# The output projection of the first two units of a retention and SwiGLU kernel, as seven products of halves

## The chip, the cores and the metric

The kernel runs on one core of a Trainium2 chip. The metric is the device time of one execution in microseconds. Before the change the median of three runs is 1154.93 us (1154.29 to 1156.06). The profile is of one more execution, with a span of 1155.2 us. A granted TensorE clock of 0.993 of full speed goes with it.

## What is computed

Eight batches of eight heads run retention over 576 positions of 64 dimensions. The result, as 4608 tokens of 512, goes through RMSNorm and a SwiGLU block of width 1536. All is float32, except that the weights arrive as float64.

```python
ret = (q @ k.T / sqrt(64)) * Dmat          # decay gamma[h] ** (i - j), causal
x = (ret @ v) -> (4608, 512)               # per batch and head, then joined
xn = x / sqrt(mean(x * x) + 1e-6) * rms_g
out = (silu(xn @ w_gate) * (xn @ w_val)) @ w_out
```

## The kernel before

**Units and pairs.** The tokens are cut into 12 units of `U` = 384. The retention is done for 32 pairs of heads; `slot(j)` holds the small matmuls of pair j (`values`, `scores`, `states`, `carried`) with VectorE's `weigh` and `sums`. Units 0 and 1 need pairs 0 to 7, which `start()` does first. From unit 2 on a main loop does, for each unit, six groups of gate and val projections (`up`), and in the last group and after it the output projection `across`, with the slots of later pairs placed between them.

**Seven products for eight.** From unit 2 on every large matrix product is taken over halves in the manner of Strassen and Winograd: seven products of halves, with sums of blocks of the activations (VectorE) and of the weights made beside them. The weight blocks are named A11, A12, A22, and S1 to S4 for combinations of quarters. For gate and val the combinations are made once, by `combine(m)` on GpSimd (L812 to L819), in `w_up[m]`, which has room for 14 block columns. For the output projection they are made by `combine_out` on VectorE, stored in DRAM as `w_blocks`, and fetched into four slots in `w_out`, in the order A11, S1, S3, S2, A12, S4, A22, as `across` needs them (`fetch`, `ORDER`).

**Units 0 and 1 are plain.** While they run, the weights still arrive as float64 and are turned into float32 by a sequence of VectorE and ScalarE steps (`rounding`, by chunks; the chunks of `w_out` are the last). `up_plain` (L554 to L573) does gate and val of both units in full products of 384 columns: four matmuls to a bank, then ScalarE's silu for gate or VectorE's multiplication into `h` for val (L570). The hidden values of unit 1 lie in `w_up[1][:, 8:]`, in the columns that `combine(1)` later overwrites with S2, S3 and S4 of val. `down(u, s)` (L575 to L584) then makes 128 tokens of the output at a time: twelve matmuls of 512 columns, a ScalarE copy, one contiguous store of 256 KB.

**The order around the change.** It is written out by hand, and each engine works its own part of it in that order: at the end of `start()`, `following(7)` (transposes of pair 8 on VectorE, loads of pair 9), stores of A11, A12 and A22, `combine(0)`, three times `down(1, s)` with the three steps of normalising unit 2 between them (`norm_0`, `norm_1` with `diagonals`, `norm_2`), `combine(1)`, `slot(8, rest=False)`, `following(8)`, three times `down(0, s)`, `slot(9)`, `following(9)`. `values(j)` ends with a tiny GpSimd memset (`tick`, L359), for which the first matmul of `carried(j)` waits. `combine_out` is spread over the 42 steps of unit 2's `up`, one operation of 128x256 to a step, 24 in all; the stores of S1, S3, S2 and S4 and the first four fetches follow it.

**`across(u)`** first makes two blocks of h on VectorE (L649: t1 = b12 - b11, then b12 = b22 - b12), 1152 columns each. Then it does product after product, each 2 x 6 matmuls of 192 columns: A11 by b11, S1 by t1, S3 by b12, S2 by b11 + b12, A12 by b21, S4 by b22, A22 by b21 less the sum. The results are added on VectorE (L646), turned by 32x32 transposes (L659) into one of three output buffers, and stored in eight transfers of 24 KB each. Its four banks come from the pool of five.

Of the kernel before, what the change touches and what calls it, by code (L numbers as in the profile page):

```python
# [14 lines left out]
P = 128  # L15
# [26 lines left out]
def kernel(  # L42
# [21 lines left out]
    U = 384  # L64
# [22 lines left out]
    def bank(name):  # L87
        return banks.tile([P, 512], F32, tag="b", name=name)
# [483 lines left out]
                    nc.scalar.activation(out=h, in_=ps[:, :U], func=AF.Silu)  # L572
                yield  # L573

    def down(u, s):  # L575
        ps = bank(f"out_{u}_{s}")
        for f in range(NF):
            nc.tensor.matmul(  # L578
                ps[:, :DM], lhsT=h_of[u][:, f, s * P : s * P + P], rhs=w_out[:, f],
                start=(f == 0), stop=(f == NF - 1),  # L580
            )
        o = outs.tile([P, DM], F32, tag="o", name=f"o_{u}_{s}")
        nc.scalar.copy(out=o, in_=ps[:, :DM])
        nc.sync.dma_start(out=out[u * U + s * P : u * U + s * P + P, :], in_=o)  # L584


    ORDER = (A11, S1, S3, S2, A12, S4, A22)
    DH = DM // 2
    w_blocks = dram.tile([7, P, NH, DH], F32, name="w_blocks")
    w_slots = w_out.rearrange("p f d -> p (f d)").rearrange("p (s f d) -> p s f d", s=4, d=DH)  # L590
    n_fetched = 0

    def quarter(row, col):

        return w_out[:, col * NH : col * NH + NH, row * DH : row * DH + DH]

    def keep(blk, t):
        nc.sync.dma_start(out=w_blocks[blk], in_=t)

    def combine_out():  # L600

        a11, a12, a21, a22 = (quarter(r, c) for r in range(2) for c in range(2))
        for c in range(NH):
            for o, a, b, op in (
                (a22, a21, a22, ALU.add), (a21, a11, a21, ALU.subtract),
                (a11, a22, a11, ALU.subtract), (a12, a12, a11, ALU.subtract),
            ):
                nc.vector.tensor_tensor(out=o[:, c], in0=a[:, c], in1=b[:, c], op=op)
                yield
        for blk, t in ((S1, a22), (S3, a21), (S2, a11), (S4, a12)):  # L610
            keep(blk, t)
        for _ in range(4):
            fetch()

    def fetch():
        nonlocal n_fetched
        if n_fetched < 7 * (NU - 2):
            nc.sync.dma_start(
                out=w_slots[:, n_fetched % 4], in_=w_blocks[ORDER[n_fetched % 7]]
            )  # L620
            n_fetched += 1

    def across(u):


        h = h_of[u]
        b11, b12 = h[:, :NH, :HU], h[:, :NH, HU:]
        b21, b22 = h[:, NH:, :HU], h[:, NH:, HU:]
        t1 = ffn.tile([P, NH, HU], F32, tag="t1", name=f"t1_{u}")
        x_, y, z, w = (bank(f"{n}o_{u}") for n in "xyzw")  # L630
        s1, u2, u4 = (temp(f"{n}o_{u}") for n in ("m1", "u2", "u4"))

        def product(rhs, ps, start):
            k = 7 * (u - 2) + n_done
            for i in range(2):
                for c in range(NH):
                    nc.tensor.matmul(  # L637
                        ps[:, i * HU : i * HU + HU],
                        lhsT=w_slots[:, k % 4, c, i * P : i * P + P], rhs=rhs[:, c],
                        start=(start and i == c == 0), stop=False, skip_group_check=True,  # L640
                    )
            if n_done < 3:
                fetch()

        def add(o, a, ps):
            nc.vector.tensor_tensor(out=o, in0=a, in1=ps[:, :U], op=ALU.add)  # L646

        def block(o, a, b, op):
            nc.vector.tensor_tensor(out=o, in0=a, in1=b, op=op)  # L649

        def result(row, col, a, ps):
            r = ps[:, :U]
            if a is not None:
                r = temp(f"c{row}{col}_{u}")
                add(r, a, ps)
            o = outs.tile([P, DM], F32, tag="o", name=f"o_{u}_{row}_{col}")[:, :U]
            end = u == NU - 1
            if not end:
                nc.vector.transpose(out=o, in_=r)  # L659
            o_of = o.rearrange("p (d t r) -> p d t r", d=2, r=SQ)  # L660
            for d in range(2):
                if end:
                    half = slice(d * HU, d * HU + HU)
                    nc.vector.transpose(out=o[:, half], in_=r[:, half])
                for i in range(P // SQ):
                    c0 = row * DH + d * P + i * SQ
                    t0 = u * U + col * HU
                    queue = nc.scalar if end and i % 2 else nc.sync
                    queue.dma_start(
                        out=out[t0 : t0 + HU, c0 : c0 + SQ].rearrange("(t c) r -> c t r", c=SQ),  # L670
                        in_=o_of[i * SQ : i * SQ + SQ, d],
                    )

        n_done = 0
        block(t1, b12, b11, ALU.subtract)
        block(b12, b22, b12, ALU.subtract)
        yield
        product(b11, x_, True)
        nc.scalar.copy(out=s1, in_=x_[:, :U])
        block(b11, b12, b11, ALU.add)  # L680
        n_done += 1
        yield
        product(t1, z, True)
        n_done += 1
        yield
        product(b12, w, True)
        n_done += 1
        yield
        product(b11, y, True)
        add(u2, s1, y)  # L690
        add(u4, u2, z)
        result(1, 1, u4, w)
        n_done += 1
        yield
        product(b21, x_, False)
        result(0, 0, None, x_)
        block(b21, b21, b11, ALU.subtract)
        n_done += 1
        yield
        product(b22, z, False)  # L700
        result(0, 1, u2, z)
        n_done += 1
        yield
        product(b21, w, False)
        result(1, 0, u2, w)
        yield
# [146 lines left out]
    def start():  # L853
# [52 lines left out]
        gather(*squares.pop())  # L906
        load_qk(2 * NHP)
        load_kv(2 * NHP)
        for m, g in [(m, g) for g in range(NG) for m in range(2)]:
            for u in range(2):  # L910
                weights_to(4 * g + 2 * m + 1)
                for i, _ in enumerate(up_plain(u, m, g)):
                    if not (u or m or g):
                        if i == 0:
                            values(2 * NHP - 1)
                            carried(2 * NHP - 1)
                            gather(1, NHP - 1, square(1, NHP - 1))
                        elif i == 1:
                            norm_1(1)
                        elif i == 2:  # L920
                            diagonals(1)
                        elif i == 3:
                            norm_2(1)
                    weights(2)
                    act(1)
                    if i == 1:
                        weights_to(4 * g + 2 * m + 2)
        following(2 * NHP - 1)
        weights_to(len(chunks))
        for blk, row, col in ((A11, 0, 0), (A12, 0, 1), (A22, 1, 1)):  # L930
            keep(blk, quarter(row, col))
        combine(0)
        for u in (1, 0):
            for s in range(NS):
                down(u, s)
                if u == 1:
                    (norm_0, norm_1, norm_2)[s](2)
                    if s == 1:
                        diagonals(2)
            if u:  # L940
                combine(1)
                slot(8, rest=False)
                following(8)
        slot(9)
# [21 lines left out]
    with tc.manual_schedule():  # L966
        start()
        for u in range(2, NU):
            made = combine_out() if u == 2 else iter(())
            for i in range(2 * NG):  # L970
                for n, _ in enumerate(up(u, i % 2, i // 2)):
                    next(made, None)
                    if n == 2 and turns:
                        prepare_next(turns.pop())
                if u > 2 and i in (1, 3):
                    fetch()
                    fetch()
                if i == 2 * NG - 1:
                    rest = across(u)
                    next(rest)  # L980
                behind(u, i)
            for i, _ in enumerate(rest):
                if i == 0 and turns:
                    prepare_next(turns.pop())
                if i == 2:
                    behind(u, 6)
                    at, n = SLOTS[u % 3]
                    if 2 * NG - 1 in at:
                        load_next(u // 3 * 8 + n + len(at) - 1)
                elif i == 4:  # L990
                    behind(u, 7)
# [27 lines left out]
```

## Time and profile before

| what | where it is read | value |
|---|---|---|
| median time | three runs | 1154.93 us |
| TensorE matmul busy | page, part 1 | 1132.9 us of 1155.2 |
| matmul, 512 columns, `down` | groups by line, L578 | 593 ns each by the record, 72 to a unit |
| matmul, 192 columns, `across` | groups by line, L637 | 326 to 329 ns each by the record |
| VectorE block of h, 128x1152 | groups by line, L649 | 1342 ns |
| VectorE weight combination, 128x256 | groups by line, L608 | 416 ns, 24 of them |
| GpSimd weight combination | groups by line, L819 | 1340 ns (gate), 1303 ns (val), 12 each |
| store of a block to `w_blocks` | transfers | 768 KB, median 6.0 us to landing |

A float32 matmul of the program stands as two records in the profile. The records overlap, so a stage is measured from one start to the next rather than by the sum of the records. In the busy time by stage the columns are start and end in us, length, then busy time and instruction count of TensorE's matmuls, its weight loads, VectorE, ScalarE and GpSimd, the granted clock, the share of the transfer engines and GB/s. In the order of time the columns are start, length, engine, line and operation, and in brackets how long the engine was idle before and what ended it.

### The profile page before, as it was taken

The numbers are of one execution on the slowest core, as the hardware profiler recorded it, in microseconds if no ns is written. First come the engines' busy times: TensorE is split into PE (matmuls) and PEld (weight loads), VectorE is DVE, ScalarE is ACT, GpSimd is POOL, SyncE is SP. The second block draws the span as 40 slices with busy tenths as digits, with TensorE's granted clock in tenths as the row PEclk, the third lists the DMA queues.
The fourth block names the chain that finished last, engine by engine and source line by source line (L and its number), as shares of the span: only waits on it lengthen the run. The fifth ranks groups of instructions, "written<-read, shape, count | busy, mean of one in ns | idle before, by whom it ended". The sixth has DMA issues, their size and how long they took to land.

```text
span 1155.2 us, 24332 instructions
## 1 busy us (share of the span) xinstructions
PE 1132.9 (98%) x10332; PEld 1025.7 (89%) x10332; DVE 696.4 (60%) x1414; ACT 246.4 (21%) x484; POOL 46.5 (4%) x74
## 2 busy tenths in 40 slices
PE   7899999999999999999999999999999999999998
PEld 6655555459999999999999999999999999999998
DVE  3888864428676575465765775465576566445352
ACT  4645641111211221111221120120220220120210
POOL 0000005500000000000000000000000000000000
PEclk8899999999999999999999999999999999999999
DMA  7945322322972656034345456306336403303304
GB/s 199 270 98 172 109 84 65 110 68 43 268 156 42 173 132 150 20 95 111 96 102 90 109 135 132 115 26 120 101 97 140 128 34 94 126 1 98 122 1 110
DMA packets 282412, 125.37 MB, mean 109 GB/s; under 512 B 257216, under 2 KB 264896, under 8 KB 282304
## 3 DMA queue, kind: packets, MB, share of 16 engines
q1 hardware_dynamic: 272688, 108.71, 37.4%
q10 hardware_dynamic: 9616, 15.11, 4.0%
q8 instruction: 81, 1.33, 0.5%
q14 instruction: 27, 0.22, 0.1%
HBM read 108.83 MB, written 14.94 MB: 107 GB/s over the span
## 4 chain that ended last, share of the span: by engine, by line
PE 91%; DVE 4%; SPq 2%; issue 1%; ACT 1%; DMA 1%; DVEq 0%; POOL 0%; POOLq 0%
PE w L507 13%; PE x L507 13%; PE z L507 13%; PE up L564 11%; PE xo L637 7%; PE wo L637 7%; PE zo L637 7%; PE y L507 6%; PE out L578 5%; PE yo L637 3%; PE av L351 2%; PE s L280 1%; PE s L300 1%; PE av L370 1%; SPq L161 1%; DVE sum L329 1%
## 5 line engine op out<-in xcount | busy, mean ns | idle before, releaser
L531 ACT COPY m<-x 128x384 f32<-128x384 f32 x60 | 28.7, 478 | 431.4 <-PE x L507 407.6
L507 PE MATMUL w<-sums,w_val 128*128 128x192 f32 x480 | 88.6, 328 | 0.4
L507 PE MATMUL z<-x,w_gate 128*128 128x192 f32 x480 | 87.9, 326 | 1.0 <-DVE u L514 1.0
L507 PE MATMUL w<-sums,w_gate 128*128 128x192 f32 x480 | 88.0, 326 | 0.8 <-DVE h L514 0.8
L507 PE MATMUL x<-x,w_val 128*128 128x192 f32 x480 | 88.7, 328 | 0.0
L507 PE MATMUL x<-x,w_gate 128*128 128x192 f32 x480 | 88.5, 328 | 0.0
L507 PE MATMUL z<-x,w_val 128*128 128x192 f32 x480 | 87.8, 326 | 0.0
L637 PE MATMUL xo<-h,w_out 128*128 128x192 f32 x480 | 82.1, 328 | 0.0
L507 PEld LDWEIGHTS w<-sums,w_val 128*128 128x128 f32 x480 | 79.2, 190 | 2.7 <-DVE c L514 2.7
L637 PE MATMUL wo<-h,w_out 128*128 128x192 f32 x480 | 81.3, 326 | 0.0
L507 PEld LDWEIGHTS z<-x,w_gate 128*128 128x128 f32 x480 | 79.6, 190 | 1.3 <-DVE u L514 1.3
L507 PEld LDWEIGHTS w<-sums,w_gate 128*128 128x128 f32 x480 | 79.4, 190 | 1.3 <-DVE h L514 1.1
L514 DVE TENSOR_TENSOR u<-m,y 128x384 f32<-128x384 f32 x60 | 33.1, 552 | 78.2 <-PE y L507 78.2
L507 PEld LDWEIGHTS x<-x,w_val 128*128 128x128 f32 x480 | 79.2, 190 | 0.6
L507 PEld LDWEIGHTS x<-x,w_gate 128*128 128x128 f32 x480 | 79.3, 190 | 0.5
L507 PEld LDWEIGHTS z<-x,w_val 128*128 128x128 f32 x480 | 79.6, 190 | 0.0
L637 PEld LDWEIGHTS xo<-h,w_out 128*128 128x128 f32 x480 | 78.1, 190 | 0.5
L637 PEld LDWEIGHTS wo<-h,w_out 128*128 128x128 f32 x480 | 78.6, 190 | 0.0
L514 DVE TENSOR_TENSOR h<-u,w 128x384 f32<-128x384 f32 x60 | 33.1, 551 | 68.9 <-PE w L507 68.9
L526 ACT ACTIVATE h<-h 128x384 f32<-128x384 f32 x90 | 47.0, 522 | 91.1 <-DVE h L514 91.1
L564 PE MATMUL up<-x,w_gate 128*128 128x384 f32 x192 | 63.3, 488 | 0.9 <-DVE x L476 0.7
L564 PE MATMUL up<-x,w_val 128*128 128x384 f32 x192 | 62.4, 486 | 0.0
(155 smaller groups left out, 1751.5 us busy)
## 6 DMA issues: line engine op xcount, KB each, us to landing
w_out<-w_blocks SPq DMA_DIRECT2D x70, 768.0 KB, 5.0
out_dram<-o SPq DMA_DIRECT2D x304, 24.0 KB, 1.6
qraw<-in_q_dram SPq DMA_DIRECT2D x96, 72.0 KB, 2.5
kraw<-in_k_dram SPq DMA_DIRECT2D x96, 72.0 KB, 3.4
k<-in_k_dram SPq DMA_DIRECT2D x48, 128.0 KB, 2.9
v<-in_v_dram SPq DMA_DIRECT2D x48, 128.0 KB, 2.8
w_blocks<-w_out SPq DMA_DIRECT2D x7, 768.0 KB, 6.0
w_out<-in_moe_w_gate_dram ACTq DMA_DIRECT2D x4, 1024.0 KB, 6.1
```

What stands on the lines that cost most here:

```text
L161: nc.sync.dma_start(out=t[:, :, e], in_=src[b, 2 * hp + e, : NFULL * P].rearrange("(c p) d -> p c d", p=P),)
L280: nc.tensor.matmul(s[side(odd), e, i * L : i * L + L], lhsT=d["kT"][side(e), c * L : c * L + L], rhs=d["qT"][side(e), c * L : c * L + L], ...
L300: nc.tensor.matmul(o[side(e)], lhsT=d["k"][side(odd), i, e], rhs=d["v"][side(odd), i, e], start=True, stop=True,)
L329: nc.vector.scalar_tensor_tensor(out=t[:, c], in0=t[:, c - 1], scalar=gc[:, hp : hp + 1], in1=part, op0=ALU.mult, op1=ALU.add,)
L351: mm = nc.tensor.matmul(av[odd][column(j, odd, e), i * L : i * L + L], lhsT=d["v"][side(odd), i, e] if c < NC - 1 else d["vt"][:, e], rhs= ...
L507: nc.tensor.matmul(ps[:, i * HU : i * HU + HU], lhsT=w_up[m][:, 2 * blk + c, cut], rhs=t_of[u][blk][:, c], start=(start and i == c == 0), ...
L514: nc.vector.tensor_tensor(out=o, in0=a, in1=pairs_of(ps), op=ALU.add)
L526: nc.scalar.activation(out=o, in_=c, func=AF.Silu)
L531: nc.scalar.copy(out=s1, in_=pairs_of(x_))
L564: nc.tensor.matmul(ps[:, :U], lhsT=w_up[m][:, 4 * half + c, i * P : i * P + P], rhs=x_of[u][:, c], start=(c == 0), stop=(c == NHP - 1),)
L578: nc.tensor.matmul(ps[:, :DM], lhsT=h_of[u][:, f, s * P : s * P + P], rhs=w_out[:, f], start=(f == 0), stop=(f == NF - 1),)
L637: nc.tensor.matmul(ps[:, i * HU : i * HU + HU], lhsT=w_slots[:, k % 4, c, i * P : i * P + P], rhs=rhs[:, c], start=(start and i == c == 0) ...
```

## The change

Units 0 and 1 get their output projection from `across` too. The seven blocks are in SBUF by then, so nothing is fetched for them: A11, A12, A22 lie in `w_out` as they came, S4 takes the place of A21 there, and S1, S3, S2 take the columns of `w_up[0]` in which gate's S2, S3, S4 are made later. `combine_out` is four operations of 128x1536 in place of 24 of 128x256. They are placed in the last group of unit 1's `up_plain`, one behind each of its four steps. Then all seven blocks are stored for the later units. `combine(0)`, which needs the columns of `w_up[0]`, moves behind unit 0's projection; `combine(1)` stays behind unit 1's. The first four fetches move into unit 2, to the places that later units have. `down` goes.

```diff
-    def down(u, s):
-        ps = bank(f"out_{u}_{s}")
...
+    first_blocks = {}
...
     def combine_out():
         a11, a12, a21, a22 = (quarter(r, c) for r in range(2) for c in range(2))
-        for c in range(NH):
-            for o, a, b, op in (
-                (a22, a21, a22, ALU.add), (a21, a11, a21, ALU.subtract),
-                (a11, a22, a11, ALU.subtract), (a12, a12, a11, ALU.subtract),
-            ):
-                nc.vector.tensor_tensor(out=o[:, c], in0=a[:, c], in1=b[:, c], op=op)
-                yield
-        for blk, t in ((S1, a22), (S3, a21), (S2, a11), (S4, a12)):
-            keep(blk, t)
-        for _ in range(4):
-            fetch()
+        s1, s3, s2 = (
+            w_up[0][:, i : i + 2].rearrange("p b f -> p (b f)").rearrange("p (f d) -> p f d", d=DH)
+            for i in (8, 10, 12)
+        )
+        for o, a, b, op in (
+            (s1, a21, a22, ALU.add), (s3, a11, a21, ALU.subtract), (s2, s1, a11, ALU.subtract),
+            (a21, a12, s2, ALU.subtract),
+        ):
+            nc.vector.tensor_tensor(out=o, in0=a, in1=b, op=op)
+            yield
+        first_blocks.update({A11: a11, A12: a12, S1: s1, A22: a22, S2: s2, S3: s3, S4: a21})
...
+            a = first_blocks[ORDER[n_done]] if u < 2 else w_slots[:, k % 4]
...
-                        lhsT=w_slots[:, k % 4, c, i * P : i * P + P], rhs=rhs[:, c],
+                        lhsT=a[:, c, i * P : i * P + P], rhs=rhs[:, c],
...
-            if n_done < 3:
+            if u > 1 and n_done < 3:
                 fetch()
...
+        made = combine_out()
...
                     act(1)
+                    if u and m and g == NG - 1:
+                        weights_to(len(chunks))
+                        next(made, None)
...
         following(2 * NHP - 1)
-        weights_to(len(chunks))
-        for blk, row, col in ((A11, 0, 0), (A12, 0, 1), (A22, 1, 1)):
-            keep(blk, quarter(row, col))
-        combine(0)
+        for _ in made:
+            pass
+        for blk, t in first_blocks.items():
+            keep(blk, t)
         for u in (1, 0):
-            for s in range(NS):
-                down(u, s)
-                if u == 1:
-                    (norm_0, norm_1, norm_2)[s](2)
-                    if s == 1:
+            for i, _ in enumerate(across(u)):
+                if u and i in (2, 4, 6):
+                    (norm_0, norm_1, norm_2)[i // 2 - 1](2)
+                    if i == 4:
                         diagonals(2)
+            combine(u)
             if u:
-                combine(1)
                 slot(8, rest=False)
                 following(8)
         slot(9)
...
-            made = combine_out() if u == 2 else iter(())
...
-                    next(made, None)
...
-                if u > 2 and i in (1, 3):
+                if i in (1, 3):
                     fetch()
                     fetch()
```

More of the change, by code (lines that the diff above doesn't have):

```diff
@@ L573, in up_plain @@
                 yield
-    def down(u, s):
-        ps = bank(f"out_{u}_{s}")
[L577 to L584, printed above, removed]
     ORDER = (A11, S1, S3, S2, A12, S4, A22)
```

## The prediction

> **What bounds the kernel now.** I read the page's busy shares and chain first, then the mean by stage, then groups by line and the order of time around the change.
>
> ```profile
> PE 1132.9 (98%) x10332; PEld 1025.7 (89%) x10332; DVE 696.4 (60%) x1414; ACT 246.4 (21%) x484; POOL 46.5 (4%) x74
> ...
> PE 91%; DVE 4%; SPq 2%; issue 1%; ACT 1%; DMA 1%; DVEq 0%; POOL 0%; POOLq 0%
> ```
>
> TensorE sets the end. Stages that differ from it must be priced on TensorE, and other engines count only where TensorE waits for them. The busy time by stage (start and end in us, length, then busy time of each engine) gives the stages that the change touches: the last projection of unit 1 with its normalisation, slot 8, the projection of unit 0, slot 9, the up stage of unit 2, its seven products, and the same two stages of unit 5.
>
> ```profile
> 190.95:223.58 32.63, 32.63 (x83) 14.73 (x81) 6.43 (x10) 3.37 (x8) 17.51 (x15) 1.00 0.45 124
> 223.58:224.78 1.20, 1.20 (x73) 1.14 (x72) 1.09 (x3) 1.20 (x5) 1.20 (x2) 1.00 0.24 92
> 224.78:255.88 31.10, 31.10 (x79) 13.60 (x72) 10.32 (x19) 1.29 (x3) 4.96 (x4) 1.00 0.26 60
> 255.88:258.17 2.29, 2.29 (x142) 2.22 (x141) 0.39 (x1) 1.87 (x5) 0.09 (x1) 1.00 0.33 113
> 258.17:322.53 64.36, 62.54 (x762) 60.96 (x756) 49.67 (x121) 13.18 (x29) 0.26 (x3) 1.00 0.59 153
> 322.53:351.25 28.72, 28.72 (x182) 28.45 (x177) 20.82 (x44) 2.28 (x6) 0.86 (x1) 1.00 0.66 136
> 530.87:592.69 61.82, 61.82 (x758) 60.94 (x757) 37.33 (x81) 13.17 (x29) 0.26 (x3) 1.00 0.40 98
> ```
>
> In both old projections TensorE is full and VectorE has 10.32 us or less in 31 us. The up stage of unit 2 is 2.54 us longer than that of unit 5: it holds the weight combinations. The waits of VectorE in order of time show where the small operations get expensive:
>
> ```profile
> 223.69 2.19 DVE L476 SCALAR_TENSOR_TENSOR x<-x,rms_g,rb 128x384 f32<-128x384 f32 x4 [7.22 <-PE rb L474]
> 225.91 1.40 DVE L487 TENSOR_TENSOR sums<-x 128x384 f32<-128x384 f32 x1
> 227.34 1.50 DVE L487 TENSOR_TENSOR x<-x 128x384 f32<-128x384 f32 x1
> 228.88 1.51 DVE L487 TENSOR_TENSOR sums<-x 128x384 f32<-128x384 f32 x1
> 230.43 0.56 DVE L487 TENSOR_TENSOR sums<-x,sums 128x384 f32<-128x384 f32 x1
> ```
>
> The first three ran beside GpSimd's weight combination (213.71 to 229.98 in the order of time), the fourth after it. In later units the same operations take 0.65 us.
>
> [...]
>
> **The change, part by part.** *Products.* A projection of 512 columns takes 31.10 us (72 matmul records). Seven products have 7 x 24 = 168 records; at the 3.90 us from one product to the next (xo at 322.53, zo at 326.54 with a restart of 0.1) that is 27.4 with the restart. With the two pieces of normalisation it is the 28.72 measured in units 2 and 5, against 32.63. Gain 3.9 + 3.7 = **7.6 us**.
>
> *Weight combinations leave the up stage of unit 2.* There the second z product began 1.3 us late behind L514, the second w product of the next group 1.15 us late, and the third group lost 0.14. In the first group, slot 9 still leaves VectorE late by about 0.8; the others go to about 0.15 and nothing. Gain **1.65 us** (bounds 1.0 and 2.54).
>
> *Four combinations go behind unit 1's last four products by h.* [...]GpSimd is then idle. Before, VectorE ended the last rounding at 184.1 with GpSimd in its way (2.05 us against 1.36); without it the first of unit 1's four multiplications begins at 185.0. Queue: 4 x 0.47 + 4 x 1.68 + the transposes of pair 8 (1.44) + the first block, t1 (1.38): t1 is there at 196.4. TensorE starts the first product at 190.95 and ends it at 194.85. The second needs t1: **stall of 1.6 us** (1.2 to 2.6). The block after it is ready by 197.8, ahead of product three at 200.3, so it is free.
>
> *The second stall.* GpSimd's combination of val reuses the columns that hold unit 1's h. It now starts in the last product of that unit, about 219.7. Products end: 190.95 + 28.72 + 1.6 = 221.3; slot 8 (1.20) to 222.5; first product of unit 0 to 226.4. VectorE gets rb at about 217.45 and must do, before unit 0's t1: everything from L476 to the transposes of pair 9, which took 223.69 to 235.56 = 11.87 before, also with GpSimd beside it; the last result's addition and transpose, 0.59 + 0.58; then t1, 1.35 alone[...]. 217.45 + 11.87 + 1.17 + 2.1 = 232.6. TensorE waits for it from 226.4: **stall of 6.2 us**. Behind t1 stand two more blocks at up to 2.2 us (the first ready by 234.8 and needed at 236.5, the second ready by 237.0 and needed at 240.4), and nothing else is late.[...]
>
> *Stores.* All seven blocks, 5.5 MB, are stored together from about 203.5. Three of them moved at 342 to 355 GB/s before, so 16 us, to 219.5. The first result of unit 1 is queued on SyncE behind them and the eighth of its eight transfers waits for the last store; it lands by about 222. Three output buffers: the fourth result, at 225, reuses it. Hidden by 3 us. The 32 small result transfers per unit are the size that later units hide.
>
> *Gate's combination moves behind unit 0.* It is ahead of slot 9's small GpSimd memset, for which the carried part of slot 9 waits. By the regions that it overwrites it may start in unit 0's third product, once val's twelve (219.7 to about 238) are done: twelve at 1.34 from 240[...]: 256.5. Slot 9 needs the memset at 256.2 + 1.7 = 257.9. Hidden, with 1.4 us to spare. The four fetches move to places where other units have them; their blocks are used 30 us later. Free.
>
> Sum: -7.6 - 1.65 + 1.6 + 6.2 = **-1.45 us**: 1154.93 to **1153.5**.
>
> **Rivals.** *The second stall is small.* [...]it is 2.9 and the sum -4.8: 1150.2. For it: GpSimd's operation is seen holding VectorE for at most 0.85. Against: L487 under the same combination was slow in every row. *The full gain.* If VectorE were never waited for, 9.25 less: 1145.7. For it: VectorE is 60% busy. Against: the slack lies in the wrong place, ahead of the last normalisation row. *Slower: a wait on stores or on the memset takes the place.* If the seven stores run at 240 GB/s (23 us), the first result lands near 229.5 and the fourth holds VectorE's queue, with t1 behind it, for about 4.5 us; with the memset 1.5 late as well, the sum is about +4: 1159. For it: the margins are 3 and 1.4 us. Against: 342 to 355 GB/s in the trace, and GpSimd was hardly slowed.
>
> **How the numbers follow.** Forecast 0.55, the small stall 0.22, the full gain 0.06, slower 0.17. 0.2% is 2.3 us. The forecast's own bounds reach from about -3.5 to +0.5, so I give 0.17 of its 0.55 to faster and 0.38 to no change. Faster: 0.17 + 0.22 + 0.06 = 0.45; within 0.38; slower 0.17. The range goes to just past the small stall and takes in the forecast with about one of the two late margins: 1149.5 to 1157.0.
>
> **What would show it.** Seven products at 3.90 us each in units 1 and 0, in 27.4 us plus waits; a wait of TensorE for the block t1 of about 1.6 us in unit 1's second product, and one of about 6 in unit 0's; L487 at 1.4 to 1.5 us there; no wait of VectorE for result transfers; no long wait for the memset in slot 9; unit 2's up stage near 62.7. A t1 of unit 0 done before 226, or a wait of VectorE on an output transfer, would make the forecast wrong, the one to the fast side, the other to the slow.

## The result, and the profile after

The changed kernel takes 1160.12 us (median of 4 runs, 1158.74 to 1162.09) against 1154.98 us before: a ratio of 1.0045, with a 95% interval of 1.0027 to 1.0063. Six more runs of it, in another session, gave 1.0041 (1.0026 to 1.0056). So it is 3 to 7 us slower. The forecast was 1153.5 us in a range of 1149.5 to 1157.0: a small gain was forecast, and the change is a loss.

The busy shares and the chain of the changed kernel, from its page, show TensorE with less to do and less of the span filled:

```profile
PE 1126.2 (97%) x10524; PEld 1053.1 (91%) x10524; DVE 716.1 (62%) x1420; ACT 243.9 (21%) x480; POOL 50.1 (4%) x74
...
PE 90%; SPq 3%; DVE 3%; DMA 2%; ACT 1%; issue 1%; DVEq 0%; POOL 0%; POOLq 0%
```

Matmul busy time fell by 6.7 us and the span of the profiled execution rose by 3.9. The busy time by stage (start and end, length, then busy time and count of TensorE's matmuls, weight loads, VectorE, ScalarE and GpSimd, granted clock, transfers) shows where. The rows are unit 1's products, slot 8, unit 0's first product and what follows it, its second product, its other five, slot 9, the up stage of unit 2, and its products:

```profile
191.77:221.65 29.88, 28.88 (x177) 28.19 (x175) 18.22 (x28) 3.63 (x9) 2.14 (x3) 1.00 0.76 229
221.65:222.96 1.31, 1.31 (x75) 1.15 (x73) 1.28 (x2) 0.00 (x0) 1.31 (x1) 1.00 0.15 23
222.96:234.32 11.36, 4.17 (x30) 3.90 (x25) 10.90 (x19) 0.48 (x1) 10.89 (x9) 0.83 0.34 52
234.32:239.79 5.47, 5.47 (x24) 5.47 (x25) 4.42 (x2) 0.00 (x0) 5.31 (x3) 0.72 0.53 87
239.79:259.29 19.50, 19.50 (x122) 19.37 (x120) 5.41 (x8) 1.50 (x4) 15.48 (x13) 1.00 0.31 57
259.29:261.63 2.34, 2.34 (x142) 2.18 (x141) 1.48 (x3) 0.00 (x0) 0.92 (x2) 1.00 0.34 53
261.63:326.05 64.42, 62.57 (x762) 61.26 (x756) 41.91 (x97) 13.18 (x29) 0.27 (x3) 1.00 0.46 109
326.05:354.77 28.72, 28.72 (x182) 28.45 (x177) 20.81 (x44) 2.28 (x6) 0.86 (x1) 1.00 0.59 133
```

From unit 1's first product to the start of unit 2's up stage, 69.86 us stand where there were 66.90 (191.27 to 258.17, from matmul to matmul). TensorE idles for 7.2 us in the third row, and the product behind it takes 5.47 us at a granted clock of 0.72; its neighbours take 3.90. Slot 9 has no wait to speak of. The up stage of unit 2 is no shorter than before, although the weight combinations are gone from it.

The order of time on VectorE and then on TensorE, at the second stall:

```profile
220.58 1.38 DVE L487 TENSOR_TENSOR sums<-x 128x384 f32<-128x384 f32 x1
221.99 1.51 DVE L487 TENSOR_TENSOR x<-x 128x384 f32<-128x384 f32 x1
223.54 1.51 DVE L487 TENSOR_TENSOR sums<-x 128x384 f32<-128x384 f32 x1
225.08 1.50 DVE L487 TENSOR_TENSOR sums<-x,sums 128x384 f32<-128x384 f32 x1
...
232.12 2.06 DVE L641 TENSOR_TENSOR t<-h 128x1152 f32<-128x1152 f32 x1
...
234.32 5.63 PE L629 MATMUL zo<-t,w_gate 128*128 128x192 f32 x24 [7.20 <-DVE t L641]
```

The block t1 of unit 0 (named t) ends at 234.18, where the second product starts. The forecast had it at 232.6, in a reckoning whose first product of unit 0 ended at 226.4; here that product ended 0.7 later (234.32 less 7.20), so t1 itself is about 1 us later than forecast. All four L487 operations now run beside GpSimd's combination of val (220.28 to 239.98), where before only three did.

In the up stage of unit 2 the order of time shows slot 11's carried part, 32 matmul records cut in two by a wait that has no releaser:

```profile
303.15 0.68 PE L370 MATMUL av<-qT,sum 64*64 64x64 f32 x27
305.15 0.33 PE L370 MATMUL av<-qT,sum 64*64 64x64 f32 x4 [1.31 <-issue]
```

### The profile page after: what moved, and what is told of

It reads as the page before. It is cut to its first block, busy times and chain, and to the rows that moved or that the text cites. A ratio compares the mean times of both kernels' runs of the same rounds, so it can differ in the third digit from the quotient of the medians.

```text
span 1159.1 us, 24792 instructions
## 1 busy us (share of the span) xinstructions
PE 1126.2 (97%) x10524; PEld 1053.1 (91%) x10524; DVE 716.1 (62%) x1420; ACT 243.9 (21%) x480; POOL 50.1 (4%) x74
## 3 DMA queue, kind: packets, MB, share of 16 engines
q8 instruction: 83, 1.36, 0.5%
## 4 chain that ended last, share of the span: by engine, by line
PE 90%; SPq 3%; DVE 3%; DMA 2%; ACT 1%; issue 1%; DVEq 0%; POOL 0%; POOLq 0%
PE x L507 13%; PE w L507 13%; PE z L507 13%; PE up L564 11%; PE zo L629 8%; PE wo L629 7%; PE xo L629 7%; PE y L507 7%; PE yo L629 4%; PE av L351 2%; PE s L280 1%; PE av L370 1%; SPq L161 1%; PE s L300 1%; DMA w_blocks<-w_out 1%
## 5 line engine op out<-in xcount | busy, mean ns | idle before, releaser
L629 PE MATMUL xo<-h,w_out 128*128 128x192 f32 x528 | 90.3, 328 | 0.0
L629 PEld LDWEIGHTS xo<-h,w_out 128*128 128x128 f32 x528 | 85.9, 190 | 0.6
L629 PE MATMUL wo<-h,w_out 128*128 128x192 f32 x504 | 85.3, 326 | 0.0
L629 PEld LDWEIGHTS wo<-h,w_out 128*128 128x128 f32 x504 | 82.5, 190 | 0.0
```

Source lines behind the costliest of these rows:

```text
L629: nc.tensor.matmul(ps[:, i * HU : i * HU + HU], lhsT=a[:, c, i * P : i * P + P], rhs=rhs[:, c], start=(start and i == c == 0), stop=False, ...
```

## The experiments

My theory after these traces had three parts: TensorE waits for t1 of unit 0, queued on VectorE and drawn out because VectorE's operations take longer beside GpSimd's combination of val (1.38 to 1.51 us for L487; the trace before has 0.56 once that combination has ended); the idle time lowers the clock, so the next product costs more again; and a pause that belongs to unit 2's fetches takes back what the moved combinations gave.

**Both kernels again.** No edit.

> The changed kernel once more, for a second trace and a narrower interval. Theory (the second stall, with a slow clock behind it): again a wait of TensorE of about 7 us for the block t1 of unit 0, and again the product behind it in about 5.5 us at a granted clock near 0.72, since both follow from the order of the instructions. The pause of 1.3 us without a shown releaser in slot 11 (TensorE, matmuls of the carried part) need not come again, since no wait belongs to it. Rival (the loss lies in the state of that one execution): wait and slow product differ from the first trace by more than 1 us. Time: 1160 under both.

> The kernel before once more, for a second trace. Theory: the stage from unit 1's projection to unit 2's first product takes 66.9 us again, as in the first trace, so that the changed kernel's 69.9 and 70.3 are its own. Pauses of TensorE without a releaser in the carried parts, 0.6 us in all in the first trace, are the part of the time that changes from execution to execution; if they sum to 2 us or more here, they are no property of the changed kernel. Time: 1155.5.

Measured: 1160.27 us for the changed kernel, against 1156.04 in its session; 1156.07 for the kernel before, against 1156.36. In the changed kernel the wait for t1 is 7.2 us again and the product behind it took 5.86 us, at 0.67. The stage from unit 1's projection to unit 2 took 70.25 us, and that of the kernel before 66.89. Busy time by stage of the second trace of each (the slow product of the changed kernel, the up stage of unit 2 of each):

```profile
234.28:240.14 5.86, 5.86 (x24) 5.86 (x25) 4.42 (x2) 0.00 (x0) 5.49 (x3) 0.67 0.72 125
```

```profile
261.98:329.88 67.90, 64.44 (x762) 63.05 (x757) 42.24 (x97) 13.17 (x29) 0.26 (x3) 0.97 0.44 104
```

```profile
256.87:321.23 64.36, 62.53 (x763) 60.97 (x757) 49.68 (x121) 13.22 (x29) 0.26 (x3) 1.00 0.58 153
```

The stall and the slow clock are there each time. The up stage of the changed kernel is not the same each time: 64.42, then 67.90 with two pauses of 1.77 and 1.16 us. The second trace is that of the slowest of its six executions (1164.57 us), so its 67.90 is not typical. I had expected that the pause need not come again; two came, and longer in sum. The kernel before had none in unit 2 in either trace. Both kernels also pause without a releaser for 1 to 5 us in the first 150 us, in amounts that change from trace to trace; that may be part of the scatter of some 2 us in the times.

**The blocks of unit 0 early.** `first_two(0)` makes t1 and the block after it, which `across(0)` then leaves out, and is called behind unit 1's third product, where VectorE idled for 7.4 us.

```diff
+    def first_two(u):
...
             for i, _ in enumerate(across(u)):
+                if u and i == 3:
+                    t1_of[0] = first_two(0)
...
```

> Unit 0's two first blocks of h are made behind unit 1's third product, where VectorE is idle for 7.4 us. Theory (TensorE waits for t1 of unit 0, queued on VectorE behind normalisation, slot 8 and pair 9): the wait of 7.2 us and the 1.57 us of the slow product are gone. But unit 0's products then end about 250.4 in the time of the changed kernel's trace, while GpSimd ends gate's combination about 255, so the memset ahead of slot 9's carried part makes TensorE wait for some 3 us that were hidden. Sum: 5.5 to 6 us faster than the changed kernel, 1154.3. Rival (the wait is for something else, such as the columns or the banks): the wait stays at about 7 us and the time at 1160.

Measured: 1153.33 us, a ratio of 0.9976 (0.9968 to 0.9984); 6.9 us faster than the changed kernel in the same session. The waits of TensorE between 180 and 260 us:

```profile
PE av L370 <- POOL tick L359: 2.8, 1, 2.8
PE zo L639 <- DVE t L621: 1.0, 1, 1.0
```

The 7.2 us are gone (the 1.0 left is unit 1's), every product of unit 0 takes 3.90, and the wait for the memset behind gate's combination has come up in slot 9, 2.8 us for the 3 expected. The rival, that the wait had been for columns or banks, falls.

**TensorE kept busy.** 22 matmuls into a bank that the third product overwrites, between unit 0's first and second product.

```diff
+        if u == 0:
+            for i in range(22):
+                nc.tensor.matmul(
+                    w[:, :HU], lhsT=first_blocks[A11][:, i % NH, :P], rhs=b21[:, i % NH],
+                    start=True, stop=True, skip_group_check=True,
+                )
         product(t1, z, True)
```

> 22 matmuls whose result is thrown away (7.15 us at 0.325 us each) stand between unit 0's first and second product, where TensorE idles for 7.4 us in the changed kernel. The output is unchanged. Theory (the idle time lowers the granted clock, and 3.1 us at half of it cost 1.57 us): the second product still starts about 234.3 and takes 3.9 us instead of 5.5; 1.5 us faster than the changed kernel, 1158.6. Rival (the product is slow because of what else runs then, GpSimd and VectorE in SBUF or the transfers): it takes 5.5 us again and the time is 1160.

Measured: 1158.41 us, 1.9 faster than the changed kernel. The filling and the second product, by stage:

```profile
224.34:231.63 7.29, 7.29 (x45) 7.01 (x44) 6.90 (x16) 0.48 (x1) 6.98 (x6) 1.00 0.32 50
231.63:235.64 4.01, 4.01 (x25) 4.01 (x25) 3.90 (x2) 0.00 (x0) 3.85 (x3) 1.00 0.72 117
```

GpSimd and VectorE were busy throughout as in the slow product (3.85 and 3.90 us of 4.01), the transfers had the same share as in the second trace (0.72), and the product took 4.01 us at full clock. So the idle time lowered the clock. In the two traces of the changed kernel it fell from 1.00 to 0.50 3.4 and 4.2 us after the last matmul, and was back at 1.00 3.0 and 3.8 us into the product. Half speed for that long loses 1.5 and 1.9 us; the product took 1.57 and 1.96 us more than 3.90.

**GpSimd's combination of val left out.** `combine(1)` is not called; the later units' val products use what is in those columns.

> The combination of val's weight blocks on GpSimd is left out (units 2 to 11 then use what lies in those columns). Theory[...]: the four operations of L487 take 0.65 us or less each instead of 1.4 to 1.5, t1 of unit 0 1.35 instead of 2.06; the wait falls from 7.2 to about 3.1 us[...], and the time by 5.7 to 1154.4. Rival (the queue alone is long[...]): the wait falls by less than 1.5 us, the clock still falls, and the time is 1158.5 or more.

Measured: 1154.86 us, 5.4 less than the changed kernel. VectorE and TensorE in order of time:

```profile
219.51 0.56 DVE L487 TENSOR_TENSOR sums<-x 128x384 f32<-128x384 f32 x1
220.10 0.56 DVE L487 TENSOR_TENSOR x<-x 128x384 f32<-128x384 f32 x1
220.69 0.56 DVE L487 TENSOR_TENSOR sums<-x 128x384 f32<-128x384 f32 x1
221.29 0.56 DVE L487 TENSOR_TENSOR sums<-x,sums 128x384 f32<-128x384 f32 x1
...
227.38 1.31 DVE L641 TENSOR_TENSOR t<-h 128x1152 f32<-128x1152 f32 x1
...
228.84 4.14 PE L629 MATMUL zo<-t,w_gate 128*128 128x192 f32 x24 [2.79 <-DVE t L641]
```

The wait falls from 7.2 to 2.8 us (2.9 is what the forecast's reckoning leaves with L487 and t1 not slowed: its 6.2 less 2.5 and 0.75), and after 2.8 us the product runs at full clock (3.98 us). So of the 8.8 us of wait and slow product, the slowing beside GpSimd made 4.4 directly and 1.5 through the clock, and the queue on VectorE the other 2.8.

**The next waits taken away.** First, with the early blocks, only the first group of gate's combination stays ahead of slot 9; then, on top, unit 1's own first blocks go ahead of S4 and the transposes of pair 8 (the first cut of the edit, in the second kernel alone).

```diff
...
-        following(2 * NHP - 1)
+        t1_of[1] = first_two(1)
         for _ in made:
             pass
+        following(2 * NHP - 1)
...
-            combine(u)
+            combine(u, range(NG) if u else (0,))
...
         slot(9)
+        combine(0, (1, 2))
...
```

> As the kernel with unit 0's early blocks, and only the first four of gate's twelve combinations stay ahead of slot 9 on GpSimd; the other eight follow it. Theory (with the blocks early, the memset behind gate's twelve combinations is the next wait): the 2.8 us that TensorE waited in slot 9 are gone, and nothing takes their place, since the second group's blocks are needed some 20 us later. 2.8 us faster than with early blocks alone: 1150.5. Rival (slot 9 waits for VectorE or for transfers anyway): under 1 us gained, 1152.5 or more.

> As the split kernel, and unit 1's two first blocks stand ahead of the fourth combination (S4) and the transposes of pair 8 on VectorE. Theory: t1 of unit 1 is there about 1.9 us before the first product ends, the wait of 1.0 us that every trace shows in unit 1's second product is gone, S4 is not needed until the sixth product; 1.0 us faster than the split kernel, 1149.5, and no wait of TensorE is left in the two units. Rival (S4 or the stores are needed sooner than thought): the wait reappears in a later product, no gain.

Measured: 1151.27 us (ratio 0.9964, 0.9952 to 0.9976) and 1149.56 us (0.9944, 0.9931 to 0.9956). Both gains are of the expected size. By stage, the second of them has unit 1's products, slot 8, unit 0's products, slot 9 and unit 2's up stage at:

```profile
191.31:219.92 28.61, 28.61 (x177) 28.21 (x175) 20.76 (x30) 3.62 (x9) 2.15 (x3) 1.00 0.72 221
219.92:221.22 1.30, 1.30 (x74) 1.14 (x72) 1.27 (x2) 0.00 (x0) 1.30 (x1) 1.00 0.97 282
221.22:248.63 27.41, 27.41 (x175) 27.27 (x168) 16.03 (x26) 1.98 (x5) 19.48 (x15) 1.00 0.45 77
248.63:250.97 2.34, 2.34 (x142) 2.18 (x141) 1.17 (x3) 0.00 (x0) 1.32 (x2) 1.00 0.32 49
250.97:315.86 64.89, 62.53 (x762) 61.21 (x757) 42.13 (x97) 13.21 (x29) 9.13 (x10) 1.00 0.49 112
```

There is no wait left in the two units. 59.66 us stand where the kernel before has 66.90: this is the gain that seven products hold here (7.2 us), and with it this kernel is faster than the kernel before and the changed one. The trace of the split kernel has two pauses in unit 2 (1.35 and 1.86 us), this one has one (1.62).

**The pause in unit 2.** Its four fetches of 768 KB were moved: all at the first of their two places, then all behind the fifth group (in the changed kernel and in the fastest one), and then left out, so that unit 2's first four products use what lies in the slots. The edit shown is the first.

```diff
-                if i in (1, 3):
-                    fetch()
-                    fetch()
+                for _ in range(4 * (i == 1) if u == 2 else 2 * (i in (1, 3))):
+                    fetch()
```

> The changed kernel with all four fetches of unit 2 at the first of the two places. Three of four traces with two fetches at each place show TensorE pausing for 1.0 to 1.3 us in the 28th matmul record of slot 11's carried part, with no releaser shown, while 1.5 MB of fetched blocks are still on the way. Theory (those transfers hold up the instructions of TensorE): that pause is gone from slot 11, or moved to slot 10, 8 us behind the fetches. Rival (the pause belongs to the place in the program, whatever the transfers do): it is there in slot 11 again. Time: 1159 under the theory, 1160.3 under the rival.

> The changed kernel with only unit 2's four fetches moved behind its fifth group. Theory: unit 2's up stage 62.7 us, against 64.4 and 67.9 in two traces of the changed kernel, so 1.5 us or more faster, 1158.6; what then is left of the loss against the kernel before is the stall with its slow clock less the products' gain, 3.2, less the 1.6 of the combinations. Rival: pauses in slots 10 or 11 as before, 1160.3.

> The kernel with both units' blocks early and gate's combination split, and unit 2's four fetches moved behind its fifth group, between slot 11 and slot 12. Theory (block transfers on the way during a slot make TensorE pause there): no pause without a releaser in unit 2, its up stage in 62.9 us instead of 64.9, and the blocks still there before the first product of unit 2 needs them; 1.6 us faster than with the fetches where they were, 1148.0. Rival (the pause belongs to the program's place): a pause of 1 to 2 us in slot 10 or 11 again, 1149.6.

> The changed kernel with unit 2's first four fetches left out (its first four products then use what lies in the slots). Theory (the pauses of 1 to 3 us in and just behind unit 2's up stage come from the fetched blocks on their way): no pause without a releaser from slot 9 to the end of unit 2's products, up stage 62.7 us and products 28.7, 2 us faster than the changed kernel, 1158.5. Rival (the pause belongs to the program, and the transfers only go before it by chance): a pause of 1 us or more in slots 10 to 12, 1160.3.

Measured: 1162.61, 1162.56, 1152.51 and 1159.48 us (ratios 1.0053, 1.0052, 0.9962 and 1.0025). The first three times were expected 3.6, 4.0 and 4.5 us too low, and are above those of the rivals too: where a fetch stands was not worth what I thought. Late fetches cost the fastest kernel 3 us in the median (1149.56 to 1152.51); its trace is that of the fastest execution (1149.32) and does not show where they go. The last time was expected 1.0 too low, but the kernel before was 0.4 to 0.8 slower in that session. By its ratio it is about 2 us faster than the changed kernel (1.0025 against 1.0041 and 1.0045), as expected, with intervals that overlap. The pause, in order of time, with all fetches at the first place (issued at 274.12):

```profile
281.24 0.56 PE L370 MATMUL av<-qT,sum 64*64 64x64 f32 x23
283.97 0.49 PE L370 MATMUL av<-qT,sum 64*64 64x64 f32 x8 [2.17 <-issue]
```

and, in the changed kernel, with all behind the fifth group. These I had meant to run between slots 11 and 12. But SyncE issued them behind the loads that stand ahead of them in the program (310.23 to 317.25), from 317.30 on, so that they ran through slot 12:

```profile
317.30 2.34 SPq L609 DMA_DIRECT2D w_out<-w_blocks x4
...
323.61 0.68 PE L370 MATMUL av<-qT,sum 64*64 64x64 f32 x30
327.17 0.26 PE L370 MATMUL av<-qT,sum 64*64 64x64 f32 x1 [2.87 <-issue]
```

The pause goes where the fetches go: from slot 11 to slot 10, and to slot 12. In the fastest kernel with late fetches it stands ahead of unit 2's first product (1.8 us). And in the one trace without the fetches there is none:

```profile
261.33:324.06 62.73, 62.19 (x762) 61.02 (x757) 41.82 (x97) 13.18 (x29) 0.27 (x3) 1.00 0.33 61
324.06:352.78 28.72, 28.72 (x183) 28.45 (x177) 20.81 (x44) 2.28 (x6) 0.86 (x1) 1.00 0.61 132
```

The up stage is then 62.73 us long, where the forecast wanted "near 62.7". So the pauses go with the fetches. But the fetches alone do not make one: the kernel with 22 more matmuls has them at the same two places, and its up stage has no pause and takes 62.73 us as well (257.48 to 320.21). One trace without a pause is therefore little by itself; the moves weigh more.

What TensorE waits for, the transfers narrow down. One queue carries what the profile calls "instruction" (q8), one packet of 0.02 MB at a time. The ten traces of the changed kernel and of those made from it, with fetches, have twelve pauses in unit 2, of 0.3 to 2.9 us. Each of the twelve ends 2.3 to 2.8 us after such a packet moved, while from the end of the block transfers it ends anywhere between 1 us before and 3 us after. In the first trace of the changed kernel the packet moved at 302.65, 1.2 us before TensorE came to the place of the pause (303.84). Without the fetches it moved at 300.3, and TensorE passed the same place at about 303.4, 3.1 us later, without a pause. So the reading that fits is that TensorE waits for its own instructions, and that these come late when blocks are on their way. It is inferred: no row says whose instructions the packet holds. That 22 more matmuls, which shift all later instructions, leave no pause would fit too. It stays open why units 3 to 11, with fetches at the same two places, have a pause only once in these traces (2.7 us, in the kernel with 22 more matmuls).

In some traces a slow clock follows a pause: the products of unit 2 behind the pause of 2.87 us ran at a mean of 0.91 and took 31.57 us instead of 28.72.

## Why the prediction was wrong

The table has the terms, as forecast and as the two traces of the changed kernel have them, in us.

| step | forecast | first trace | second trace |
|---|---|---|---|
| seven products for the projections | -7.6 | -7.4 | -7.4 |
| wait for t1 of unit 1 | +1.6 | +1.0 | +1.0 |
| wait for t1 of unit 0 | +6.2 | +7.2 | +7.2 |
| slow clock behind that wait | 0 | +1.6 | +2.0 |
| restarts, slots 8 and 9 | 0 | +0.6 | +0.6 |
| combinations out of unit 2 | -1.65 | -1.6 | -1.6 |
| pauses in unit 2, clock included | 0 | +1.7 | +5.2 |
| sum | -1.45 | +3.1 | +7.0 |

The products' term is 28.61 and 27.41, the lengths without waits, less 32.31 and 31.10, all from matmul to matmul (the forecast's 32.63 began 0.3 earlier, at a weight load). The pauses' term is 64.42 and 67.90 less 62.73, and the combinations' 62.73 less 64.36. The sums answer to 69.86 + 64.42 and 70.25 + 67.90 against 66.90 + 64.36, which is +3.0 and +6.9, and the ratio says 3 to 7.

- **Right:** the products' gain; that the block t1 of each unit would be waited for (unit 1's came at 196.8, 0.4 later than forecast, and TensorE began 0.8 later, so that 1.0 was left of 1.6); what stands ahead of it on VectorE; that VectorE is slower beside GpSimd's combination (L487 1.38 to 1.51 us, t1 of unit 0 2.06, for which the forecast had 2.1, its 1.35 alone and 0.75 for GpSimd beside it; t1 of unit 1, with GpSimd idle, took 1.32); that stores and the memset would stay hidden (the last store and unit 1's first result landed at about 222, as forecast; the memset by 0.7 us instead of 1.4); that the combinations cost unit 2 1.65 us. The 1.68 us for each of the four combinations of 128x1536, a shape that the trace before lacks, was an estimate of mine; they took 1.75 us each, and 1.67 from one to the next operation.
- **Wrong, first: "stall of 6.2 us", and nothing after it.** The size was 7.2, because a fourth L487 operation ran beside GpSimd's combination (1.50 us instead of 0.56). The larger error is what was left out: this stall lowered the clock, from 1.00 to 0.50. Wait and slow product together are 8.8 and 9.2. The forecast read a wait as costing its own length. The work behind 7.2 us ran at half clock for 3.0 and 3.8 us, and the work behind 2.8 us, in the kernel without GpSimd's combination of val, did not.
- **Wrong, second: the fetches, called "Free".** I argued from the time at which their blocks are used. What goes with them on TensorE while they move was not in the sum: 1.7 and 5.2 us. The profile before had no such pause in unit 2; what it did show was that its four fetches stood at another place. That they set off the pauses is shown by the moves; how they do so is inferred.
- **The rivals.** The slower one named waits on stores or on the memset. Both stayed hidden; the memset became the bound only when the stall in front of it was removed (2.8 us). A wait of VectorE for a result transfer was named as a sign against the forecast. The profile does put 1.5 us of VectorE's idle time before 251.69 down to one, but the product that is turned there ended at 251.65 by the record, so it held nothing up. The small stall and the full gain were wrong for this kernel. The rearranged kernel has the whole gain of the products and no wait in the two units. Its ratio of 0.9944 puts it at 1148.5 from 1154.93, still 2.8 us above 1145.7; its up stage of unit 2, 64.89 us instead of 62.73, is 2.2 of them.
- **Readings that were off.** The 0.65 us "in later units" is the mean of all rows of L487 with the three slow ones in it, and 1.36 is such a mean too; the later rows take 0.56 and the other roundings 1.22. Start to start, the two late products of unit 2 were 1.14 and 1.01 late, not 1.3 and 1.15. The loss does not come from these.

With the slow clock in it (+1.6) the forecast's sum would have been about +0.15, and with the pauses of the first trace (+1.7) about +1.85; the rest to +3.1 is the stall's missing 1.0 and smaller terms.

## What to carry to other kernels

When one engine's work is cut down, look at what the next piece of it needs and what stands ahead of that in the other engine's queue: making two operations some 30 us sooner in VectorE's order was worth 6.9 us, nearly as much as the seven products save in the projections (7.4 us). A wait of TensorE as long as this one must be priced with the slow clock behind it, 1.6 and 2.0 us here on top of 7.2. Background transfers may be late for nobody and still not be free: of the places tried here none was better in the median than the one that the change gave them.

## What the runs showed that I had not expected

- Pauses of TensorE of 0.3 to 2.9 us with no releaser went with 3 MB of block transfers, and each ended 2.3 to 2.8 us after a packet of the queue called "instruction". There were none in unit 2 in the trace without these transfers, and none in the kernel before and in the one with 22 more matmuls, which have them.
- Both sides were slower beside each other: GpSimd's twelve operations of val took 16.27 us before, beside three of the slow L487 operations, and 19.70 us in the changed kernel, beside four of them and three blocks of 1152 columns. Those blocks took 2.06 to 2.30 us there, and 1.32 alone.
- The length of a wait alone does not say whether the clock falls. Behind runs of small 64x64 matmuls it fell to 0.50 with pauses of 1.77 us (second trace of the changed kernel, 0.50 from 286 to 289 us, behind the pause that ended at 285.15) and 2.17 us, but not with 1.86 us (split kernel) or with the 2.8 us of slot 9 in the kernel with early blocks. Behind a full product, 2.8 us did not lower it.
